# First four attention groups of a fused attention and two-MLP kernel: products with v by chunks of 32 keys in four PSUM banks, a new start order, one load of mem_v

## The chip, the cores and the metric

The kernel runs on one core of one Trainium2 chip. The metric is the device time of one execution in microseconds (us). Before the change it was 1058.13 us, the median of three runs (1057.98 to 1058.34).

## What is computed

Attention over chunks: 4 sequences, 8 heads, 768 tokens, 64 values a head. Each chunk of 32 queries sees its own 32 keys, 16 to the left, 8 to the right and 8 memory keys, so 64 keys in all. Two MLPs follow on the 3072 tokens.

```python
for c in range(nc):                               # chunks of 32 queries
    k_full = np.concatenate([mem_k, k_ctx], axis=2)
    v_full = np.concatenate([mem_v, v_ctx], axis=2)
    scores = scale * np.matmul(q_c, k_full.transpose(0, 1, 3, 2))
    a = np.exp(scores - np.max(scores, axis=-1, keepdims=True))
    a = a / (np.sum(a, axis=-1, keepdims=True) + 1e-09)
    out[:, :, c_start:c_end] = np.matmul(a, v_full)
h = x @ w_in                                      # 512 to 2048
x = np.where(h > 0.0, h, np.exp(np.minimum(h, 0.0)) - 1.0) @ w_out
y = ((x @ w1) * (x @ w2)) @ w3 @ w_out2
```

## The kernel before, in words

The work goes in 24 groups of 128 queries (four chunks, eight heads). Six matrices' worth of weights come as 64-bit numbers and are taken apart into a high and a low 32-bit part on ScalarE and VectorE; a product of such parts is three matmuls (`mm3`, lines 130 to 133). The first MLP runs by blocks of 512 tokens, which is four groups. So before the first matmul of the first MLP (`mm_h(0)`, lines 602 to 608) the first four groups (0 to 3) must have gone through attention. This start is written out by hand in the string `START` (line 72): a letter is a step, a digit its group, and every engine executes its instructions in the order in which the string issues them.

The steps of a group: `t` (351) transposes q and k on TensorE and copies them to SBUF; `s` (372) multiplies them to scores, 32 matmuls that the trace shows as 64 records; `m` (391) takes the maximum and subtracts it on VectorE, then exponentiates on ScalarE; `z` (400) sums and inverts; `n` (411) multiplies by the inverse; `p` (423) transposes by blocks of 32 on VectorE; `v` (429) multiplies with v; `o` (439) splits the result into a cast (ScalarE, line 127) and a remainder (VectorE, line 128) for the MLP. `k` and `w` ask for the q, k and v of a group on the SyncE queue (299 to 328), and the `l` steps ask for weights (147, 155). A group's v comes as one load of 128 tokens (line 321), four of 24 tokens (325) and, in groups 0 to 2, four of the 8 memory values (328, on the GpSimd queue).

In `n` the probabilities of 32 keys are written twice, once as they are and once as zeros, with the factors `rc` that line 406 makes with the mask `odd`. So `p` moves 1024 elements a partition, and `v` takes the keys in two blocks of 64 rows, for two chunks at a time, the zeros cancelling the other chunk's keys: 32 matmuls of 64 rows, 64 columns of v and 64 moving columns (64 records).

The weights go through `Feed` (204 to 263). One `act` (letter `a`) does on ScalarE the high part of job i-2 (line 179), the rebase of job i (166) and its top bits (188); one `dve` (letter `d`, in two halves `x` and `y`) does on VectorE the low part of job i-3 (182) and the merge of job i-1 (192). `act` also asks for the load of a later job. `mm_h(0)` needs both parts of job 0, and line 914 issues the steps that are still missing. The letters `i` and `j` are 6 matmuls each whose result nobody reads (`busy`, 595), shown as 12 records each.

PSUM has eight banks: `PA` (two), a pair for group 1 and one for group 2, and `PS[4]`, `PS[5]`. After the start the pairs' room becomes `PS[0]` to `PS[3]`. Groups 1 and 2 have their own SBUF tiles.

Of the kernel before, what the change touches and what calls it, by code (L numbers as in the profile page):

```python
# [8 lines left out]
F32 = mybir.dt.float32  # L9
# [4 lines left out]
ALU = mybir.AluOpType  # L14
# [6 lines left out]
def tile_kernel(  # L21
# [23 lines left out]
    nc = tc.nc  # L45
    P = 128
    B, H, S, D = q.shape
    NM = mem_k.shape[2]
    CH, LEFT, RIGHT = 32, 16, 8
    WIN = LEFT + CH + RIGHT  # L50
    KEYS = WIN + NM
    NCG = 4
    GQ = NCG * CH
    GPS = S // GQ
    NG = B * GPS
    HP = H // 2
    DM = H * D
    KT = DM // P
# [4 lines left out]
    EARLY = 3  # L63
# [5 lines left out]
    LATER = (11, 12, 13, 14, 15, 27, 28, 29, 30, 31)  # L69
    SHARED = {2: 24, 3: 25, 4: 26}  # L70

    START = "u0 t0 b1 k3 w1 l2 w2 s0 m0 t1 b2 s1 z0 n0 m1 t2 p0 v0 w3 l4 l6 c s2 z1 n1 o0 m2 p1 t3 v1 k4 s3 z2 n2 p2 o1 a d a m3 d v2 i z3 j n3 p3 o2 a d x v3 o3 a y w4"
    SCALE = 1.0 / float(D) ** 0.5
    assert GQ == P and KEYS == 64 and KT == 4 and HP == 4 and DM == 512

# [2 lines left out]
    psum = ctx.enter_context(tc.tile_pool(name="psum", bufs=1, space=PSUM))  # L78
# [5 lines left out]
    ident = const.tile([P, P], F32, name="ident")  # L84
    xhl = [const.tile([P, 2, KT, TB], F32R, name=f"xhl{i}") for i in range(2)]
# [1 line left out]
    for i, j in SHARED.items():  # L87
        W[j] = W[i]
    PA = psum.tile([P, 2, 512], F32, name="banks")
    PS = [None if i < KT else psum.tile([P, 512], F32, name=f"bank{i}") for i in range(6)]  # L90
    early_psum = ctx.enter_context(ExitStack())
    pb_p = early_psum.enter_context(tc.tile_pool(name="pb_p", bufs=1, space=PSUM))
    PB = [pb_p.tile([P, 2, 512], F32, name=f"pair{i}") for i in range(EARLY - 1)]

    w3d = [[dram.tile([P, 2, 512], F32, name=f"w3d{h}_{c}") for c in range(FF2)] for h in range(2)]
    wod = [dram.tile([P, 2, 512], F32, name=f"wod{c}") for c in range(FF2)]
# [21 lines left out]
    mm = nc.tensor.matmul  # L118
# [154 lines left out]
    def at_tile(G, pool, shape, name, tag=None):  # L273
        tag = tag or name
        if 0 < G < EARLY:
            pool, tag = early_p, f"{tag}{G}"
        return pool.tile(shape, F32, tag=tag, name=name, bufs=1)
# [8 lines left out]
    odd = at_tile(0, at_p, [GQ, 2, 1], "odd")  # L286

    def banks(G):
        return PB[G - 1] if 0 < G < EARLY else PA

    def small(shape, name):
        return at_p.tile(shape, F32, tag=name, name=name, bufs=2)
# [1 line left out]
    def by_token(src, b, t0, t1):  # L294
        return src[b, :, t0:t1, :].rearrange("h s d -> s h d")
# [3 lines left out]
    def load_qk(G):  # L299
        if G >= NG:  # L300
            return
        b, g = divmod(G, GPS)
        t0 = g * GQ + RIGHT
        n = min(P, S - t0)
        kn_g = k_t[G] = at_tile(G, qk_p, [P, H, D], "kn") if 0 < G < EARLY else kn
        q_t[G] = at_tile(G, qk_p, [GQ, H, D], "qn")
        if g == 0:
            nc.sync.dma_start(out=head[0:RIGHT], in_=by_token(k, b, 0, RIGHT))
            nc.sync.dma_start(out=head[RIGHT:RIGHT + NM], in_=by_token(mem_k, b, 0, NM))
        eng = nc.scalar if G == 0 else nc.sync  # L310
        eng.dma_start(out=q_t[G], in_=by_token(q, b, g * GQ, (g + 1) * GQ))
        nc.sync.dma_start(out=kn_g[0:n], in_=by_token(k, b, t0, t0 + n))

    def load_v(G):
        if G >= NG:
            return
        b, g = divmod(G, GPS)
        t0 = g * GQ - LEFT
        p0 = max(0, -t0)
        vw_g = v_t[G] = at_tile(G, v_p, [P, 2, H, D], "vw") if 0 < G < EARLY else vw  # L320
        nc.sync.dma_start(out=vw_g[p0:P, 0], in_=by_token(v, b, t0 + p0, t0 + P))
        for c in range(NCG):
            t1 = t0 + (c + 1) * CH
            n1 = min(LEFT + RIGHT, S - t1)
            nc.sync.dma_start(out=vw_g[c * CH:c * CH + n1, 1], in_=by_token(v, b, t1, t1 + n1))
            if g == 0 or G < EARLY:
                eng = nc.gpsimd if G < EARLY else nc.sync
                eng.dma_start(out=vw_g[c * CH + LEFT + RIGHT:(c + 1) * CH, 1], in_=by_token(mem_v, b, 0, NM))

    def bank(G, r, b):  # L330
        return banks(G)[:, r, 0:HP * b].rearrange("p (a b) -> p a b", b=b)
# [18 lines left out]

    def at_turn(G):
        qn, kn, pq, pk = q_t.pop(G), k_t.pop(G), bank(G, 0, GQ), bank(G, 1, P)
        for hp in range(HP):
            nc.tensor.transpose(pq[:, hp, :], pair(qn, hp), ident)  # L354
        for hp in range(HP):
            nc.tensor.transpose(pk[:, hp, :], pair(kn, hp), ident)  # L356
        qT = at_tile(G, at_p, [P, HP, GQ], "qT", "qp")
        if G not in kT_t:
            at_border(G)
        kT = kT_t[G]  # L360
        blocks = pk.rearrange("p a (c k) -> p a c k", k=CH)
        copy_on("v" if G < 2 else "a", qT, pq)
        nc.scalar.copy(kT[:, :, :, FRONT:WIN], blocks)
        nc.scalar.copy(kT[:, :, 1:NCG, 0:FRONT], blocks[:, :, 0:NCG - 1, CH - FRONT:CH])
        if G % GPS < GPS - 1:
            nc.scalar.copy(front[:, :, 0, :], blocks[:, :, NCG - 1, CH - FRONT:CH])
        qT_t[G] = qT
# [32 lines left out]
    def at_sum(G):  # L400
        rc = small([GQ, 2, 2 * HP], "rc")
        sm = small([GQ, 1, 2 * HP], "sm")
        nc.vector.tensor_reduce(out=sm, in_=e_t[G], axis=AX, op=ALU.add)
        nc.vector.tensor_scalar_add(sm, sm, 1e-9)
        nc.vector.reciprocal(out=sm, in_=sm)
        nc.vector.tensor_tensor(
            out=rc, in0=sm.to_broadcast([GQ, 2, 2 * HP]), in1=odd.to_broadcast([GQ, 2, 2 * HP]), op=ALU.mult
        )
        e_t[G] = e_t[G], rc

    def at_norm(G):
        e, rc = e_t[G]
        e2 = at_tile(G, at_p, [GQ, 2 * HP, 2, 2, CH], "e2", "qp")
        for s in range(2):
            nc.vector.tensor_tensor(
                out=e2[:, :, :, s, :],
                in0=e.rearrange("p r a (u k) -> p (r a) u k", u=2),
                in1=rc[:, s].rearrange("p (a u k) -> p a u k", u=1, k=1).to_broadcast([GQ, 2 * HP, 2, CH]),
                op=ALU.mult,
            )  # L420
        e_t[G] = e2

    def at_flip(G):
        e2 = e_t.pop(G)
        pT = at_tile(G, at_p, [P, 2, HP, 2, 2 * CH], "pT", "ke")
        nc.vector.transpose(out=pT.rearrange("p r a u i -> p (r a u i)"), in_=e2.rearrange("p a u s k -> p (a u s k)"))  # L426
        pT_t[G] = pT

    def at_values(G):
        pT, vw, px = pT_t.pop(G), v_t.pop(G), banks(G)  # L430
        for hp in range(HP):
            for u in range(2):
                for c in range(2):
                    cc = slice(c * D, (c + 1) * D)
                    for r in range(2):
                        o = px[r * D:(r + 1) * D, c, hp * D:(hp + 1) * D]
                        mm(o, lhsT=vw[cc, u, 2 * hp + r, :], rhs=pT[cc, r, hp, u, :], start=u == 0, stop=u == 1)  # L437

    def at_out(G):
        px = banks(G)[:, :, 0:2 * GQ].rearrange("p x (a t) -> p x a t", a=HP)  # L440
        j, g = divmod(G, GPB)
        hi, lo = (
            xhl[j % 2][:, i, :, g * GQ:(g + 1) * GQ].rearrange("p a (x t) -> p x a t", x=2) for i in range(2)
        )
        split(hi, lo, px)

# [123 lines left out]
    for G in range(GPB, NG):  # L570
        s0 = base(G)
# [22 lines left out]

    def busy(x, times):
        for _ in range(times):
            mm(PS[5][0:2 * H, 0:P], lhsT=x, rhs=ident, start=True, stop=True)

    h_t, eg_t, g_t = {}, {}, {}
    seq = [(j, f, f, f == FF1 - 1) for j in range(NB) for f in range(FF1)]  # L600
# [220 lines left out]
    with tc.manual_schedule():  # L821
# [10 lines left out]
        first_late = min(due[i] for i in LATER)  # L832
        feed = Feed(jobs)

        nc.gpsimd.memset(front, 0.0)
        load_qk(0)
        nc.scalar.copy(memo, front[:, :, :, 0:NM])
        make_identity(nc, ident)
        nc.gpsimd.memset(vw[0:LEFT, 0], 0.0)
        for c in range(NCG):  # L840
            for s in range(2):
                nc.gpsimd.memset(odd[c * CH:(c + 1) * CH, s], float(c % 2 == s))
        load_qk(1)
        load_qk(2)
        load_v(0)
        one = dict(t=at_turn, b=at_border, u=at_first, s=at_scores, m=at_max, z=at_sum, n=at_norm, p=at_flip, v=at_values, o=at_out, k=load_qk, w=load_v)
        for what in START.split():
            if what == "a":
                feed.act()
            elif what == "d":  # L850
                feed.dve()
            elif what == "x":
                feed.low_part()
            elif what == "y":
                feed.merge_part()
            elif what == "i":
                busy(ident[:, 0:2 * H], 6)
            elif what == "j":
                busy(e_t[3][1].rearrange("p s a -> p (s a)"), 6)
            elif what == "c":  # L860
                feed.cap = len(jobs)
            elif what[0] == "l":
                feed.cap = int(what[1])
                feed.load(feed.cap)
            else:
                one[what[0]](int(what[1]))
        assert feed.at == feed.acted
        early_psum.close()
        psum_x = ctx.enter_context(tc.tile_pool(name="psum_x", bufs=1, space=PSUM))
        for i in range(KT):  # L870
            PS[i] = psum_x.tile([P, 512], F32, name=f"bank{i}")
        NH = NB * FF1
        for n in range(NH + 2):
# [173 lines left out]
```

## Time and profile before

| | |
|---|---|
| median of three runs | 1058.13 us (1057.98 to 1058.34) |
| the profiled execution, its own time | 1057.77 us |
| its span, first to last instruction | 1056.0 us |
| TensorE busy over the span | 1033.5 us (98%) |
| VectorE, ScalarE busy | 566.8 us (54%), 458.6 us (43%) |
| GpSimd busy | 8.5 us, all in the first 10 us |
| first matmul of the first MLP | 36.31 us after the start |

The profiled execution lies 0.36 us below the median. TensorE is the bound over nearly all of the span, and its idle time lies at the start and at the very end; all that the diff touches lies in the first 37 us. So the question is at what time the dense part begins. A line of a timeline gives the start, the length, the engine, the line of the kernel, the operation, the tiles and shapes and how many instructions were merged; in brackets stands the idle time before it and what ended that.

### The profile page before, as it was taken

The page shows a single profiled execution, that of the slowest core. Times are in us where ns is not written, and L with a number is a line of the kernel's source. Part 1 is how long each engine was busy: PE and PEld are TensorE (multiplying, and loading weights), DVE is VectorE, ACT ScalarE, POOL GpSimd, SP SyncE. Part 2 cuts the span into 40 slices and gives each one's busy share as a digit, 9 for nine tenths or more (in the row PEclk, how much of TensorE's full clock was granted, in tenths as well). Part 3 has the DMA queues.
Part 4 walks back from the last instruction along what each step waited for, and adds up shares of the span by engine and source line. Part 5 has one row for each costly group of instructions (what it writes and reads, how often), then busy time and mean ns, then how long its engine had stood idle before and what let it go on. Part 6 is the DMA issues. An engine that isn't in the chain of part 4 may idle for free.

```text
span 1056.0 us, 19258 instructions
## 1 busy us (share of the span) xinstructions
PE 1033.5 (98%) x7784; PEld 884.8 (84%) x7784; DVE 566.8 (54%) x989; ACT 458.6 (43%) x890; POOL 8.5 (1%) x28
## 2 busy tenths in 40 slices
PE   5899999999999999999999999999999999999997
PEld 4678888888888888888888888899999999999996
DVE  6898856657665756666572324144444444444323
ACT  4888755545555555455543332122222223222222
POOL 3000000000000000000000000000000000000000
PEclk9999999999999999999999999999999999999999
DMA  9998648565856675667536645554475466546521
GB/s 179 268 268 250 185 141 264 158 208 179 239 161 210 194 219 183 205 193 236 163 140 212 238 159 160 174 182 162 151 271 169 157 216 231 162 141 220 169 70 61
DMA packets 178005, 199.19 MB, mean 189 GB/s; under 512 B 101404, under 2 KB 142620, under 8 KB 177916
## 3 DMA queue, kind: packets, MB, share of 16 engines
q1 hardware_dynamic: 176348, 197.36, 60.3%
q8 instruction: 62, 1.02, 0.4%
q10 hardware_dynamic: 1184, 0.39, 0.1%
q0 software_dynamic: 384, 0.20, 0.1%
q14 instruction: 27, 0.22, 0.1%
HBM read 154.93 MB, written 42.99 MB: 187 GB/s over the span
## 4 chain that ended last, share of the span: by engine, by line
PE 95%; DVE 2%; ACT 2%; DMA 1%; issue 0%; SPq 0%; DVEq 0%; ACTq 0%
PE bank L131 21%; PE bank L133 20%; PE bank L132 20%; PE bank L740 7%; PE bank L741 7%; PE bank L739 7%; PE banks L437 2%; PE banks L133 2%; PE banks L132 2%; PE banks L131 2%; PE banks L378 2%; PE banks L356 1%; PE banks L354 1%; PE banks L472 1%; DMA raw<-in_moe_w_in_dram 0%; DVE pT L426 0%
## 5 line engine op out<-in xcount | busy, mean ns | idle before, releaser
L131 PE MATMUL bank<-xhl,w 128*128 128x512 f32 x384 | 153.9, 401 | 1.0 <-ACT xhl L127 1.0
L131 PE MATMUL bank<-g,w 128*128 128x512 f32 x384 | 153.3, 399 | 0.0
L133 PE MATMUL bank<-g,w 128*128 128x512 f32 x384 | 150.0, 391 | 0.0
L132 PE MATMUL bank<-xhl,w 128*128 128x512 f32 x384 | 149.8, 390 | 0.2 <-DVE xhl L128 0.2
L133 PE MATMUL bank<-xhl,w 128*128 128x512 f32 x384 | 150.0, 391 | 0.0
L132 PE MATMUL bank<-g,w 128*128 128x512 f32 x384 | 149.8, 390 | 0.0
L612 ACT ACTIVATE eg<-bank 128x512 f32<-128x512 f32 x96 | 57.3, 597 | 116.1 <-PE bank L133 115.8
L618 DVE SCALAR_TENSOR_TENSOR eg<-eg,bank 128x512 f32<-128x512 f32 x96 | 65.6, 684 | 66.3 <-ACT eg L613 66.3
L504 DVE TENSOR_TENSOR e<-bank,e 128x384 f32<-128x384 f32 x64 | 35.7, 558 | 119.2 <-PE bank L741 119.2
L131 PEld LDWEIGHTS bank<-xhl,w 128*128 128x128 f32 x384 | 72.1, 188 | 16.1 <-ACT xhl L127 1.1
L131 PEld LDWEIGHTS bank<-g,w 128*128 128x128 f32 x384 | 72.1, 188 | 15.6
L133 PEld LDWEIGHTS bank<-xhl,w 128*128 128x128 f32 x384 | 72.1, 188 | 15.6
L133 PEld LDWEIGHTS bank<-g,w 128*128 128x128 f32 x384 | 72.1, 188 | 15.3
L132 PEld LDWEIGHTS bank<-xhl,w 128*128 128x128 f32 x384 | 72.2, 188 | 14.5 <-DVE xhl L128 0.5
L132 PEld LDWEIGHTS bank<-g,w 128*128 128x128 f32 x384 | 72.2, 188 | 14.3 <-DVE g L626 0.3
L626 DVE TENSOR_TENSOR g<-eg,g 128x512 fp32r<-128x512 f32 x96 | 65.9, 686 | 21.7 <-ACT g L622 21.5
L740 PE MATMUL bank<-xd,w 128*128 128x384 f32 x224 | 75.8, 338 | 0.0
L622 ACT CAST g<-eg 128x512 fp32r<-128x512 f32 x96 | 59.7, 622 | 28.2 <-DVE eg L618 28.0
L504 DVE TENSOR_TENSOR e<-bank,eg 128x384 f32<-128x384 f32 x64 | 35.7, 557 | 58.8 <-PE bank L741 58.8
L741 PE MATMUL bank<-xd,w 128*128 128x384 f32 x192 | 64.7, 337 | 0.0
L739 PE MATMUL bank<-xd,w 128*128 128x384 f32 x192 | 64.2, 334 | 0.0
L613 ACT ACTIVATE eg<-eg 128x512 f32<-128x512 f32 x96 | 60.7, 633 | 3.1
(173 smaller groups left out, 1855.1 us busy)
## 6 DMA issues: line engine op xcount, KB each, us to landing
w<-wqd SPq DMA_DIRECT2D x96, 512.0 KB
raw<-in_moe_w_dram SPq DMA_DIRECT2D x32, 512.0 KB
w<-shd SPq DMA_DIRECT2D x30, 512.0 KB
wqd<-st SPq DMA_DIRECT2D x24, 512.0 KB
raw<-in_moe_w_out_dram SPq DMA_DIRECT2D x22, 512.0 KB
w3d<-st SPq DMA_DIRECT2D x16, 512.0 KB
w<-w3d SPq DMA_DIRECT2D x16, 512.0 KB
w<-wqd SPq DMA_DIRECT2D x32, 256.0 KB
```

Source lines behind the costliest of these rows:

```text
L131: mm(o, lhsT=w_hi, rhs=x_hi, start=start, stop=False)
L132: mm(o, lhsT=w_hi, rhs=x_lo, start=False, stop=False)
L133: mm(o, lhsT=w_lo, rhs=x_hi, start=False, stop=stop)
L504: nc.vector.tensor_tensor(out=o, in0=a, in1=b, op=op)
L612: nc.scalar.activation(e, h_t[n], AF.Relu, scale=-1.0)
L613: nc.scalar.activation(e, e, AF.Exp, scale=-1.0)
L618: nc.vector.scalar_tensor_tensor(out=e, in0=e, scalar=-1.0, in1=h_t.pop(n), op0=ALU.add, op1=ALU.max)
L622: nc.scalar.copy(g_t[n][:, 0, :], eg_t[n])
L626: nc.vector.tensor_tensor(out=g[:, 1, :], in0=eg_t.pop(n), in1=g[:, 0, :].bitcast(F32), op=ALU.subtract)
L739: mm(o, lhsT=args[0], rhs=args[2], start=start and i == 0, stop=False, skip_group_check=more)
L740: mm(o, lhsT=args[0], rhs=args[3], start=False, stop=False, skip_group_check=more)
L741: mm(o, lhsT=args[1], rhs=args[2], start=False, stop=i == 1, skip_group_check=more)
```

## The change

1. `v` in groups 0 to 3: the probabilities stay as they are, without zeros. `n` is one multiply of 512 elements, `p` transposes 512 elements, line 406 is gone, and `v` multiplies each chunk of 32 keys for itself: 64 matmuls of 32 rows, 64 columns of v and 32 moving columns, each chunk into a bank of its own (`PV`, four banks shared by the four groups). The output is read from four banks.
2. PSUM: groups 0 and 2 use `PA`, groups 1 and 3 one pair `PB`. The transposed q of groups 0 and 1 goes to `PV`, that of 2 and 3 stays beside k. `PS[4]` and `PS[5]` come only after the start, and the matmuls of `i` and `j` write to `PA`.
3. mem_v is loaded once (four loads on the ScalarE queue), into the tile of group 1, which VectorE clears first; GpSimd copies it to the tiles of groups 0 and 2. The twelve loads on the GpSimd queue are gone.
4. Order: `p0` stands before `m1`, `p1` before `o0`; one `a d` less stands before `m3`, so that each remaining `a` and `d` works on an earlier job, and the missing step is issued by line 914 just before `mm_h(0)`; `n3` stands before `j`, which now reads the result of `n3`.

```diff
-    START = "u0 t0 b1 k3 w1 l2 w2 s0 m0 t1 b2 s1 z0 n0 m1 t2 p0 v0 w3 l4 l6 c s2 z1 n1 o0 m2 p1 t3 v1 k4 s3 z2 n2 p2 o1 a d a m3 d v2 i z3 j n3 p3 o2 a d x v3 o3 a y w4"
+    START = "u0 t0 b1 k3 w1 l2 w2 s0 m0 t1 b2 s1 z0 n0 p0 m1 t2 v0 w3 l4 l6 c s2 z1 n1 p1 o0 m2 t3 v1 k4 s3 z2 n2 p2 o1 a m3 d v2 i z3 n3 j p3 o2 a d x v3 o3 a y w4"
...
-    PS = [None if i < KT else psum.tile([P, 512], F32, name=f"bank{i}") for i in range(6)]
+    PS = [None] * 6
...
-    PB = [pb_p.tile([P, 2, 512], F32, name=f"pair{i}") for i in range(EARLY - 1)]
+    PB = pb_p.tile([P, 2, 512], F32, name="pair")
+    PV = pb_p.tile([P, NCG, 512], F32, name="four")
...
-        return PB[G - 1] if 0 < G < EARLY else PA
+        return PB if G in (1, EARLY) else PA
...
+    def load_mem_v(eng, vw_g, b, c):
+        eng.dma_start(out=vw_g[c * CH + LEFT + RIGHT:(c + 1) * CH, 1], in_=by_token(mem_v, b, 0, NM))
...
-            if g == 0 or G < EARLY:
-                eng = nc.gpsimd if G < EARLY else nc.sync
-                eng.dma_start(out=vw_g[c * CH + LEFT + RIGHT:(c + 1) * CH, 1], in_=by_token(mem_v, b, 0, NM))
+            if g == 0 and G:
+                load_mem_v(nc.sync, vw_g, b, c)
...
+        if G < 2:
+            pq = PV[:, G].rearrange("p (a b) -> p a b", b=GQ)
...
+        if G <= EARLY:
+            e2 = e_t[G] = at_tile(G, at_p, [GQ, 2 * HP, 2, CH], "e2", "qp")
+            nc.vector.tensor_tensor(
+                out=e2,
+                in0=e.rearrange("p r a (u k) -> p (r a) u k", u=2),
+                in1=rc.rearrange("p s (a u k) -> p (s a) u k", u=1, k=1).to_broadcast([GQ, 2 * HP, 2, CH]),
+                op=ALU.mult,
+            )
+            return
...
+        if G <= EARLY:
+            for hp in range(HP):
+                for u in range(2):
+                    for c in range(NCG):
+                        cc = slice(c * CH, (c + 1) * CH)
+                        for r in range(2):
+                            o = PV[r * D:(r + 1) * D, c, hp * CH:(hp + 1) * CH]
+                            mm(o, lhsT=vw[cc, u, 2 * hp + r, :], rhs=pT[cc, r, hp, u, :], start=u == 0, stop=u == 1)
+            return
...
-            mm(PS[5][0:2 * H, 0:P], lhsT=x, rhs=ident, start=True, stop=True)
+            mm(PA[0:2 * H, 0, 0:P], lhsT=x, rhs=ident, start=True, stop=True)
...
+        vw_early = [vw] + [at_tile(G, v_p, [P, 2, H, D], "vw") for G in range(1, EARLY)]
+        nc.vector.memset(vw_early[1][:, 1], 0.0)
...
+        for c in range(NCG):
+            load_mem_v(nc.scalar, vw_early[1], 0, c)
...
+        for i in (0, 2):
+            nc.gpsimd.tensor_copy(vw_early[i][:, 1], vw_early[1][:, 1])
...
-                busy(e_t[3][1].rearrange("p s a -> p (s a)"), 6)
+                busy(e_t[3].rearrange("p a u k -> p (a u k)")[:, 0:2 * H], 6)
...
-        for i in range(KT):
+        for i in (4, 5, 0, 1, 2, 3):
             PS[i] = psum_x.tile([P, 512], F32, name=f"bank{i}")
```

## Rows read from the trace of the kernel before

**Rows 1.** Windows: busy time and instructions by engine, then clock, DMA share, GB/s.

```profile
...
120.00:200.00 80.00, 80.00 (x722) 65.10 (x722) 51.99 (x95) 43.24 (x84) 0.00 (x0) 1.00 0.60 182
...
```

**Rows 2.** The chain of work that ended last, in order of time, 0 to 70 us.

```profile
...
29.40 5.10 DMA raw<-in_moe_w_in_dram
...
48.53 0.69 DVE f L192
...
59.34 1.28 PE banks L437 x64
...
```

**Rows 3.** Timeline of PE, 0 to 62 us.

```profile
...
19.45 0.86 PE L378 MATMUL pair<-kT,qT 64*32 64x64 f32 x64
...
23.58 2.22 PE L437 MATMUL pair<-pT,vw 64*64 64x64 f32 x64 [1.38 <-DVE pT L426]
25.74 1.18 PE L378 MATMUL banks<-kT,qT 64*32 64x64 f32 x64
...
29.26 1.03 PE L437 MATMUL pair<-pT,vw 64*64 64x64 f32 x52 [0.31 <-DMA vw<-in_v_dram]
30.22 1.48 PE L597 MATMUL bank<-ident 128*16 128x128 f32 x12
31.54 1.47 PE L597 MATMUL bank<-ident,rc 128*16 128x128 f32 x12
34.04 1.28 PE L437 MATMUL banks<-pT,vw 64*64 64x64 f32 x64 [1.03 <-DVE pT L426]
36.31 0.50 PE L131 MATMUL bank<-xhl,w 128*128 128x512 f32 x1 [0.99 <-ACT xhl L127]
...
40.84 0.66 PE L356 MATMUL banks<-ident,kn 128*128 128x128 f32 x4 [0.39 <-DMA kn<-in_k_dram]
...
```

**Rows 4.** Groups of instructions by line and shape, 0 to 37 us: busy us, mean ns.

```profile
...
L415 DVE TENSOR_TENSOR e<-e,rc 128x512 f32<-128x512 f32 x8 | 5.2, 688 | 0.1
L426 DVE STREAM_TRANSPOSE pT<-e 128x1024 f32<-128x1024 f32 x4 | 5.0, 1240 | 0.1
...
```

**Rows 5.** Timeline of ACT, 0 to 62 us.

```profile
...
0.75 0.43 ACTq L311 DMA_DIRECT2D qn<-in_q_dram  x1
...
34.52 0.71 ACT L166 ACTIVATE f<-raw 128x512 f32<-128x512 f32 x1 [3.09 <-DMA raw<-in_moe_w_in_dram]
...
35.67 0.59 ACT L127 CAST xhl<-banks 128x512 fp32r<-128x512 f32 x1
36.13 0.64 ACT L179 CAST w<-f 128x512 fp32r<-128x512 f32 x1
...
49.42 0.67 ACT L166 ACTIVATE f<-raw 128x512 f32<-128x512 f32 x1
...
```

**Rows 6.** DMA queues, 0 to 50 us (packets, MB, share), and the issues by line.

```profile
...
q0 software_dynamic: 384, 0.20, 2.8%
...
vw<-in_mem_v_dram POOLq DMA_DIRECT2D x12, 16.0 KB, 5.2
...
```

**Rows 7.** Windows of 4 us, the columns of rows 1.

```profile
...
8.00:12.00 4.00, 3.02 (x72) 2.51 (x72) 1.55 (x3) 1.39 (x5) 1.85 (x4) 1.00 1.37 182
...
20.00:24.00 4.00, 1.82 (x50) 1.42 (x36) 3.97 (x6) 1.65 (x6) 0.00 (x0) 0.98 0.88 264
24.00:28.00 4.00, 3.18 (x128) 2.80 (x127) 3.83 (x9) 3.05 (x7) 0.00 (x0) 0.59 0.84 174
28.00:32.00 4.00, 3.16 (x80) 2.74 (x74) 3.65 (x8) 2.39 (x5) 0.00 (x0) 1.00 0.61 141
...
```

**Rows 8.** Timeline of DVE, 0 to 62 us.

```profile
...
7.17 0.69 DVE L124 COPY qT<-banks 128x512 f32<-128x512 f32 x1 [7.17 <-PE banks L356]
...
32.74 1.25 DVE L426 STREAM_TRANSPOSE pT<-e 128x1024 f32<-128x1024 f32 x1
...
```

**Rows 9.** Timeline of POOL, 0 to 62 us.

```profile
...
1.38 0.51 POOL L839 MEMSET vw<- 16x512 f32 x1
...
```

**Rows 10.** Timeline of the SyncE queue, 0 to 62 us.

```profile
...
8.98 2.67 SPq L325 DMA_DIRECT2D vw<-in_v_dram  x4
...
```

More of the change, by code (lines that the diff above doesn't have):

```diff
@@ L319, in load_v @@
         p0 = max(0, -t0)
-        vw_g = v_t[G] = at_tile(G, v_p, [P, 2, H, D], "vw") if 0 < G < EARLY else vw
+        vw_g = v_t[G] = vw_early[G] if G < EARLY else vw
         nc.sync.dma_start(out=vw_g[p0:P, 0], in_=by_token(v, b, t0 + p0, t0 + P))
@@ L405, in at_sum @@
         nc.vector.reciprocal(out=sm, in_=sm)
+        if G <= EARLY:
+            e_t[G] = e_t[G], sm
+            return
         nc.vector.tensor_tensor(
@@ L424, in at_flip @@
         e2 = e_t.pop(G)
+        if G <= EARLY:
+            pT = pT_t[G] = at_tile(G, at_p, [P, 2, HP, 2, CH], "pT", "ke")
+            nc.vector.transpose(out=pT.rearrange("p r a u i -> p (r a u i)"), in_=e2.rearrange("p a u k -> p (a u k)"))
+            return
         pT = at_tile(G, at_p, [P, 2, HP, 2, 2 * CH], "pT", "ke")
@@ L430, in at_values @@
         pT, vw, px = pT_t.pop(G), v_t.pop(G), banks(G)
+        if G <= EARLY:
+            for hp in range(HP):
[5 more added lines that the diff above has]
+                            mm(o, lhsT=vw[cc, u, 2 * hp + r, :], rhs=pT[cc, r, hp, u, :], start=u == 0, stop=u == 1)
+            return
         for hp in range(HP):
@@ L439, in at_out @@
     def at_out(G):
-        px = banks(G)[:, :, 0:2 * GQ].rearrange("p x (a t) -> p x a t", a=HP)
+        n = NCG if G <= EARLY else 2
+        px = (PV if G <= EARLY else banks(G))[:, :, 0:DM // n].rearrange("p x (a t) -> p x a t", a=HP)
         j, g = divmod(G, GPB)
         hi, lo = (
-            xhl[j % 2][:, i, :, g * GQ:(g + 1) * GQ].rearrange("p a (x t) -> p x a t", x=2) for i in range(2)
+            xhl[j % 2][:, i, :, g * GQ:(g + 1) * GQ].rearrange("p a (x t) -> p x a t", x=n) for i in range(2)
         )
```

## The prediction, made blind

> **What bounds the kernel now.** I read the windows first. From 120 to 200 us TensorE is busy 80.00 of 80.00 us [rows 1], so nothing that the change does can be seen there: it can only move the time at which this dense part begins. Then I read the chain of waits. It goes through a weight's transfer from 29.40 to 34.5 us, then without a gap through ScalarE to 48.5 us, through VectorE, and reaches TensorE with the product with v of group 4 at 59.34 us [rows 2]. So between 34.5 and 59 us not TensorE but the ScalarE and VectorE work is late, and a step that moves on ScalarE at 36 us moves the whole rest. Last I read the timelines of the start. TensorE's second product (group 2) runs its last part only at 29.26 us, when the last of its v has landed [rows 3]. VectorE is busy nearly without a break: 3.97, 3.83 and 3.65 of 4 us [rows 7].
>
> **VectorE, part by part.** The multiply by the inverse is done eight times in the four groups, 688 ns each; four of them go, 2.75 us. The transpose takes 1240 ns for 1024 elements [rows 4]; for 512 I take half and a little, 0.65 us (bounds 0.62 and 1.24), so 4 x 0.59 = 2.4 us go. With the four small mask products that makes some 5 us. Group 3's transpose, which began at 32.74 us [rows 8], would end near 29. It doesn't follow that the start ends 5 us earlier: group 2's v still lands where the transfers let it, and what is late next is that transfer. So I cost the VectorE saving at nothing. The earlier q and k copies (PV lets VectorE and ScalarE read different tiles) save under 1 us before the first scores and go to the same wait. Clearing the one v tile (0.2 to 0.7 us) lies in VectorE's idle 7.17 us at the start [rows 8].
>
> **The transfers.** Twelve loads of 16 KB go, 0.20 MB [rows 6], and four come, 0.066 MB. The queues run full there: the DMA share is 1.37 and 182 GB/s are moved [rows 7]. 0.131 MB at 182 GB/s are 0.72 us; by the number of packets it is a little more, and I take 0.8 us (bounds 0 and 1.5) by which all later loads land earlier. The four issues on ScalarE cost 0.43 us each [rows 5], 1.7 us in a stretch in which it waits for the first transposes. The two GpSimd copies are of 512 elements; its clearing of 512 took 0.51 us [rows 9], and I take 0.5 to 1.2 us each. They must end before SyncE may ask for the tails of v (line 325), first at 8.98 us [rows 10]; mem_v is asked for by about 5 us and took 5.2 us to land on the old queue [rows 6]. A wait of a microsecond or two there is covered by the loads that are already queued.
>
> **The products.** Each has 128 records in place of 64. Nothing in the trace has 32 rows. The nearest row is the scores: 64 columns move, over eight places in the array as in the new product, and 64 records take 0.86 us, 13.4 ns each [rows 3]. The old product has four places and takes 1.28 us, 20 ns each [rows 3]. I take 13.4 ns, so 1.72 us a product: 0.44 us dearer than before. Bounds are 10 ns (less streams in each) and 20 ns (each record costs what it cost).
>
> [...]
>
> **The path to the first MLP.** Group 2's v has landed at 29.26 - 0.8 = 28.46 us. Behind it are 112 of 128 records: 1.50 us, to 29.96. Then `i` and `j`, which run from 30.22 to 33.01 us, 2.79 us [rows 3], stand ahead of group 3's product: that starts at 32.75 instead of 34.04. (Its wait for the bank that group 2's cast and remainder read, 1.3 us, and its transposed input are covered by `i` and `j`; so is the later `n3`.) It ends at 34.47, and its cast starts at 34.53, 1.14 us earlier than the 35.67 of before [rows 5].
>
> Now the moved `a d`. Before, rebase and top bits of the third job stood ahead of the cast, from 34.52 us, and the high part of the second job followed at 36.13 [rows 5]. After, behind the cast come the high part of the first job, then rebase and top bits of the third, then the second's high part. The same three plus one more: 34.53 + 0.46 + 0.52 + 1.15 = 36.66 us instead of 36.13, **0.5 us later** on the ScalarE chain that the rest hangs on. VectorE gets one merge and one low part between the cast and the third matmul of the first MLP, which comes near 37.0; the first stood at 36.31 [rows 3]. TensorE itself would be ready: group 4's keys, for which it waited until 40.84 [rows 3], land earlier too. But the gain there is lost in the wait for ScalarE. The weights' loads that `act` asks for come one step later, so one goes behind group 4's five loads of v on the SyncE queue. Its rebase stands at 49.42 us [rows 5], some 10 us after the asking, and I cost the delay at nothing (up to 0.5 us if that cover is gone).
>
> **The clock.** [...] After, TensorE is done with group 3's scores by some 24.3 us (25.74 + 1.18 = 26.92 before [rows 3], less half of VectorE's 5 us) and has next to nothing until v lands at 28.46. [...]
>
> **The sum,** at the end of the ScalarE work that stands around group 3's cast: -0.8 (v lands earlier), +0.54 (behind it 1.50 us of the second product instead of 30.22 - 29.26 = 0.96), -1.03 (no wait between `j` and group 3's product, 33.01 to 34.04), +0.15 (that product and the step to its cast, 1.78 instead of 1.63), which is the cast's -1.14; +0.52 (one more high part behind the cast), +1.15 (rebase and top bits behind it instead of ahead): +0.5. With 0.4 for the clock: +0.9 us. The profiled execution took 1057.77 us, 0.36 below the median; set against the median, 1058.13 + 0.9 = **1059.0 us**. A measurement of this kernel tells 0.2%, 2.1 us, from no change, so the forecast is no difference.
>
> **Rivals.** (a) *The clock stays down over `i` and `j`* (slower). [...] It decides if the low clock lasts beyond about 31 us. [...] Against it: before, the clock was back while TensorE ran one product and one set of scores. 15%.
> (b) *A record of the product costs 20 ns whatever its size* (slower). The two products on the path take 112 x 20 and 128 x 20 ns, 0.74 and 0.84 us more than summed: +2.1 to +2.5, 1060.4. The scores speak against it; that they load 32 columns of weights and the product 64 speaks for it. 12%. [...]
> (c) *Transfers and products both at their good ends* (faster). 1.5 us earlier and 10 ns a record: 0.7 and 0.8 us off the 0.5, -1.0 us: 1057.1. It decides if group 2's v lands by 27.8 us. Against it: only 0.13 MB go. 20%, with 4% for more than 2.1 us.
> (d) *SyncE waits for the GpSimd copies* until the queued loads run dry (slower). I put those at 3 us (an estimate: the first four tails alone took 2.67 us to ask for [rows 10]); if the copies end after 12 us, each further microsecond moves all loads: about +1, 1060.0. 7%.
>
> **The numbers.** The forecast has 46%, with its own range 1057.9 to 1060.0. Slower by over 0.2%: most of (a) and half of (b), with a little of (d) and of the forecast, 20%. Faster by over 0.2%: 4%. The range reaches from (c) without its far end to (a) with a clock that returns late: 1056.9 to 1061.3.
>
> **What would show it.** Right: in the changed profile group 2's product waits for a transfer of v near 28.5 us, group 3's transpose is done before 30, group 3's product follows `j` without a wait, and the chain still reaches group 4's product, near 60 us, through ScalarE. The three steps are shown wrong by a product that takes over 2.2 us at the full clock, by v landing at 29.2 as before, or by group 4's product earlier than 59. A first MLP matmul before 34 us would make the whole prediction wrong.

## The result: slower, by more in most runs than in the profiled one

The changed kernel took 1064.07 us in the median of six runs (1060.83 to 1066.74), the kernel before 1058.03: a ratio of 1.0056, interval 1.0047 to 1.0066, some 6 us. That is outside the predicted range (1056.9 to 1061.3). The kernel before stays within 1.1 us over its six runs, the changed one spreads over 5.9. The profiled execution, 1060.83 us, is the fastest of the six, so its profile shows about half of the usual loss: +3.06 us against the profiled execution before.

The first section of the profile's page after, here for TensorE: 256 matmul records more than the 7784 of before, four groups with 64 each (and as many weight loads).

```profile
PE 1037.9 (98%) x8040; PEld 888.7 (84%) x8040; DVE 562.9 (53%) x982; ACT 458.8 (43%) x890; POOL 2.9 (0%) x18
```

The timeline of TensorE after, which answers to [rows 3]:

```profile
16.35 1.95 PE L459 MATMUL four<-pT,vw 32*64 32x32 f32 x128
18.48 0.86 PE L383 MATMUL banks<-kT,qT 64*32 64x64 f32 x64 [0.18 <-ACT front L371]
...
22.66 1.01 PE L359 MATMUL pair<-ident,qn 128*128 128x128 f32 x4 [3.32 <-issue]
...
24.46 2.47 PE L459 MATMUL four<-pT,vw 32*64 32x32 f32 x128
26.86 1.18 PE L383 MATMUL pair<-kT,qT 64*32 64x64 f32 x64
28.36 1.10 PE L459 MATMUL four<-pT,vw 32*64 32x32 f32 x55 [0.32 <-DVE xhl L129]
30.15 1.34 PE L459 MATMUL four<-pT,vw 32*64 32x32 f32 x73 [0.70 <-issue]
31.42 2.56 PE L628 MATMUL banks<-ident 128*16 128x128 f32 x12
33.81 1.47 PE L628 MATMUL banks<-ident,e 128*16 128x128 f32 x12
35.22 0.45 PE L459 MATMUL four<-pT,vw 32*64 32x32 f32 x30
35.95 1.18 PE L459 MATMUL four<-pT,vw 32*64 32x32 f32 x98 [0.28 <-issue]
```

Look at the idle times marked "issue": 3.32, 0.70 and 0.28 us in which the profile shows nothing that TensorE waited for. Two of them cut a product in the middle. Now count between them. Beside each matmul record the trace has a record of its weight load, so 128 matmul records are 256 records in all. From 22.66 to the cut at 30.15: 4 + 4 (group 3's k, not in the fence) + 128 + 64 + 55 = 255 matmul records, 510 with the weight loads. From there to the cut at 35.95: 73 + 12 + 12 + 30 = 127, so 254. So the cuts lie 254 records and twice 255 apart; I call what lies between two such places a block. The profile's list of DMA queues agrees: in q8, which it marks "instruction", from 0 to 40 us, four transfers of 16 KB before, six after. Over the whole execution they are 62 before and 64 after, two more for TensorE's 512 records more, so 256 records a transfer; the other queue with that mark, q14, has 27 in both.

```profile
q8 instruction: 4, 0.07, 0.8%
```

```profile
q8 instruction: 6, 0.10, 1.3%
```

The windows after, with the columns of [rows 1], show a second thing, the granted clock (third column from the end). It is at 0.50 from 20 to 32 us, where before only 24 to 28 us lay low (mean 0.59 [rows 7]), and low again under the first MLP matmuls (mean 0.57 from 40 to 44 us).

```profile
20.00:24.00 4.00, 1.34 (x7) 1.34 (x7) 3.08 (x7) 0.99 (x3) 0.00 (x0) 0.50 0.93 278
24.00:28.00 4.00, 3.96 (x195) 3.22 (x193) 1.30 (x3) 2.53 (x6) 0.00 (x0) 0.50 0.72 139
28.00:32.00 4.00, 2.98 (x134) 2.59 (x132) 3.08 (x7) 1.80 (x4) 0.00 (x0) 0.50 0.89 257
32.00:36.00 4.00, 3.72 (x61) 2.75 (x58) 2.14 (x4) 1.24 (x3) 0.00 (x0) 0.79 0.83 265
40.00:44.00 4.00, 4.00 (x12) 3.03 (x13) 2.97 (x5) 4.00 (x9) 0.00 (x0) 0.57 1.04 300
```

The path then goes as the prediction read it, through ScalarE. First group 3's cast and the first exponent step of the MLP after (line 643), then that step before (line 612):

```profile
37.27 0.58 ACT L128 CAST xhl<-four 128x512 fp32r<-128x512 f32 x1 [4.03 <-PE four L459]
...
44.35 0.58 ACT L643 ACTIVATE eg<-bank 128x512 f32<-128x512 f32 x1
```

```profile
41.07 0.58 ACT L612 ACTIVATE eg<-bank 128x512 f32<-128x512 f32 x1
```

And group 4's product with v comes at 62.73 us instead of 59.34 [rows 2], +3.39, of which the span keeps 3.0:

```profile
62.73 1.28 PE L467 MATMUL banks<-pT,vw 64*64 64x64 f32 x64 [0.53 <-DVE pT L447]
```

### The profile page after: what moved, and what is told of

Its sections match the earlier page's. It is cut to its first block, busy times and chain, and to the rows that moved or that the text cites. A ratio compares the mean times of both kernels' runs of the same rounds, so it can differ in the third digit from the quotient of the medians.

```text
span 1059.0 us, 19734 instructions
## 1 busy us (share of the span) xinstructions
PE 1037.9 (98%) x8040; PEld 888.7 (84%) x8040; DVE 562.9 (53%) x982; ACT 458.8 (43%) x890; POOL 2.9 (0%) x18
## 4 chain that ended last, share of the span: by engine, by line
PE 95%; DVE 2%; ACT 2%; issue 1%; DMA 0%; SPq 0%; ACTq 0%; DVEq 0%
PE bank L132 21%; PE bank L134 20%; PE bank L133 20%; PE bank L771 7%; PE bank L772 7%; PE bank L770 7%; PE banks L467 2%; PE banks L134 2%; PE banks L133 2%; PE banks L132 2%; PE banks L383 2%; PE banks L361 1%; PE banks L359 1%; PE banks L503 1%; PE four L459 1%
```

## The experiments

Two theories to tell apart: the *supply* of TensorE's instructions, which the doubled records of the products outrun, and the *order* of the start (with the shared banks), whose moved `a d` was the cost that the prediction had named. Each ratio is against runs of the kernel before on the same chip. The edits are abridged: `...` and comments stand for what is left out.

### Old products, all else changed (e1)

```diff
-        if G <= EARLY:      # sums, multiply, transpose, product by 32 keys
-            ...
+        # the old path: 64 rows with zeros, 64 records, two banks of PV
```

> The changed kernel with the old products in groups 0 to 3 (64 rows with zeros, 64 records a group, two of the four banks of PV); order, PSUM, the one load of mem_v stay changed. Supply theory (TensorE's instructions come in blocks of 256 records, and the doubled records of the products outrun them): the stretch without work ahead of group 3's transposes (19.3 to 22.7 us) shrinks to under 1 us, group 4's product comes before 60 us, and the time is 1057 to 1059 us. Order theory (the moved a d and the shared banks cost the time): still 1060 or more.

Measured: 1061.06 us, ratio 1.0028 (1.0017 to 1.0039), within 0.7 us over six runs. The spread is gone and group 3's transposes follow the scores without a stretch; one cut of 0.69 us is left, inside group 1's product. But 3 us remain, and group 4's product comes at 62.25 us: so neither theory has it all. The cast starts 1.27 us later than before (35.67 [rows 5]). As the timelines read, with `p0` and `p1` moved forward nothing fills VectorE's wait for the exponents, and group 3's product then waits 0.97 us for group 2's remainder. From the cast to line 620, the exponent step, 7.06 us pass instead of 5.40, which is the moved `a d`.

```profile
36.94 0.59 ACT L128 CAST xhl<-four 128x512 fp32r<-128x512 f32 x1 [4.15 <-PE four L444]
...
44.00 0.57 ACT L620 ACTIVATE eg<-bank 128x512 f32<-128x512 f32 x1
```

### The kernel before with its records doubled (e2)

```diff
-                        o = px[r * D:(r + 1) * D, c, hp * D:(hp + 1) * D]
-                        mm(o, lhsT=vw[cc, u, 2 * hp + r, :], rhs=pT[cc, r, hp, u, :], start=u == 0, stop=u == 1)
+                        # groups 0 to 3, for h in range(2), outside u
+                        o = px[r * D:(r + 1) * D, c, hp * D + h * CH:hp * D + (h + 1) * CH]
+                        mm(o, lhsT=vw[cc, u, 2 * hp + r, :], rhs=pT[cc, r, hp, u, h * CH:(h + 1) * CH], start=u == 0, stop=u == 1)
```

> The kernel before, with each product of groups 0 to 3 issued as two matmuls of 32 moving columns instead of one of 64: the same arithmetic, rows and zeros, 128 records a group instead of 64, nothing else changed. Supply theory: stretches without work open on TensorE at every 256th record, between 19 and 36 us, the clock falls for longer, and the time goes up by 2 to 7 us. Order theory: at most 1 us, for the products' own length.

Measured: 1070.46 us, ratio 1.0112 (1.0099 to 1.0125), +12.6 us: more than the supply theory's upper end. The records' own length explains a part of it: group 3's product took 2.07 us for 128 records instead of 1.28, so four products cost some 3 us. The cuts are where the count puts them:

```profile
31.68 0.64 PE L440 MATMUL pair<-pT,vw 64*64 64x32 f32 x12 [0.85 <-issue]
32.25 1.18 PE L378 MATMUL banks<-kT,qT 64*32 64x64 f32 x64
33.36 1.70 PE L440 MATMUL pair<-pT,vw 64*64 64x32 f32 x50
38.67 2.35 PE L440 MATMUL pair<-pT,vw 64*64 64x32 f32 x78 [3.61 <-issue]
40.96 2.74 PE L608 MATMUL bank<-ident 128*16 128x128 f32 x12
```

12 + 64 + 50 = 126 matmul records, 252 with the weight loads, so nearly one block; then 3.61 us of nothing inside group 2's product. Only the number of records and their length (32 moving columns instead of 64) were changed here. (`i` took 2.74 us, nearly twice its 1.48 of [rows 3], though this profile's windows from 0 to 120 us show the clock at 1.00 throughout; that is left open.)

### The changed kernel with half of its records (e8)

```diff
-                for u in range(2):
+                for u in range(1):
...
-                            mm(o, lhsT=vw[cc, u, 2 * hp + r, :], rhs=pT[cc, r, hp, u, :], start=u == 0, stop=u == 1)
+                            mm(o, lhsT=vw[cc, u, 2 * hp + r, :], rhs=pT[cc, r, hp, u, :], start=True, stop=True)
```

> The changed kernel with the products of groups 0 to 3 leaving out the second 32 keys (64 records a group instead of 128); VectorE, order, PSUM, loads as changed. Leaves out part of the sum over keys. Supply theory: no stretch without work over 1 us ahead of group 3's transposes, the runs lie within 1 us of one another, and what is left is what the blind prediction summed without the third cost, 1058 to 1060 us. If the stalls had another cause than the number of records, the time stays at 1061 to 1067 with the same spread.

Measured: 1058.62 us, ratio 0.9998 (0.9989 to 1.0007). The 6 us are gone with half of the records, VectorE, order and loads being as changed. The runs spread over 3 us (1057.45 to 1060.49), not 1, but so did 29 runs of the kernel before on this chip, over 2.7. One cut of 1.11 us is left inside group 1's product. Its profile comes nearest to what the prediction had in mind:

```profile
26.86 1.17 PE L459 MATMUL four<-pT,vw 32*64 32x32 f32 x64 [2.30 <-DMA vw<-in_v_dram]
27.96 2.74 PE L628 MATMUL banks<-ident 128*16 128x128 f32 x12
30.49 2.24 PE L628 MATMUL banks<-ident,e 128*16 128x128 f32 x12
32.66 0.86 PE L459 MATMUL four<-pT,vw 32*64 32x32 f32 x64
```

Group 2's product waits for v, and v is there at 26.86 us, 2.4 us earlier than before. Around and after that wait the clock is low (mean 0.65 from 24 to 28 us, 0.50 from 28 to 32), and `i` and `j` take 4.77 us instead of 2.79. The kernel also leaves out the work of those records, about 0.9 us a product at 13.4 ns each, so not all of its 6 us are waiting.

### The stretch follows the count (e10)

```diff
+        busy(ident[:, 0:2 * H], 10)
         for what in START.split():
```

> The changed kernel with ten matmuls more (40 records, results unread) at the very start, where TensorE waits for the first keys. Supply theory: the stretches without work stand where the 256-record blocks end, so each moves 40 records forward: the one before group 3's transposes (record 706 of the changed profile) now lies inside group 2's scores, about 40 of their 128 records from the end; the time stays at 1061 to 1067. If the stretch belonged to the transposes (a wait for data or a bank), it stays where it was.

Measured: 1064.29 us, ratio 1.0059 (1.0045 to 1.0072). The stretch left the transposes and now cuts group 2's scores, 19 matmuls (38 records) from their end, and the transposes follow at once:

```profile
18.45 0.69 PE L383 MATMUL banks<-kT,qT 64*32 64x64 f32 x45
23.94 0.63 PE L383 MATMUL banks<-kT,qT 64*32 64x64 f32 x19 [4.80 <-issue]
24.50 1.11 PE L359 MATMUL pair<-ident,qn 128*128 128x128 f32 x4
```

In the start of the kernel before, no set of scores shows a wait once it has begun (64 records in 0.86 and in 1.18 us, without a gap [rows 3]). So the stretch belongs to the place in the instruction stream and not to a step. The other profiles agree: counted from the start of the program, every cut marked "issue" inside a step stands at matmul record 221, 346 to 349, 472 to 476, 598 to 603 or 730, whatever step is there. (The mark "issue" alone is not enough: the kernel before has 1.02 us of it ahead of group 0's product, which starts at 18.01 us, when VectorE's transpose has just ended.)

Beside the stretches stand the packets of q8 in the traces, the blocks counted as above. Times in us:

| stretch ends in | block's end before it crossed | next transfer of 16 KB starts | has landed | TensorE goes on |
|---|---|---|---|---|
| changed, group 3's transposes | 17.45 | 18.55 | 21.33 | 22.66 |
| changed, group 2's product | 26.49 | 27.62 | 28.73 | 30.15 |
| e2, group 2's product | 31.68 | 36.30 | 37.35 | 38.67 |
| e4, group 2's product | 27.84 | 33.16 | 34.09 | 35.62 |
| e10, group 2's scores | 17.46 | 21.20 | 22.23 | 23.94 |

Each transfer starts only after the last block's end was crossed. At all such cuts in the profiles TensorE goes on 0.8 to 1.8 us after a transfer has landed. Most transfers take 0.9 to 1.6 us (three took 2.2 to 2.9); what varies most is how long after the crossing they start, 0.8 to 5.3 us. So I read the stretches as TensorE's wait for that transfer.

### The order: old order with the new products (e5) and with the old ones (e6)

```diff
-    START = "... z0 n0 p0 m1 t2 v0 ... z1 n1 p1 o0 m2 t3 v1 ... o1 a m3 d v2 i z3 n3 j p3 ..."
+    START = "... z0 n0 m1 t2 p0 v0 ... z1 n1 o0 m2 p1 t3 v1 ... o1 a d a m3 d v2 i z3 n3 j p3 ..."   # e5; e6 has j n3
```

> The changed kernel with the start order of before (only n3 stays ahead of j). Supply theory: the stretches without work on TensorE stay, the runs still spread by 3 us or more, and the time is about 1.5 to 3 us under the changed kernel's, which is the order's own cost: 1061 to 1063. If the order alone were the cause: 1057 to 1058.

Measured: 1065.14 us, ratio 1.0055 (1.0042 to 1.0067): the old order gives nothing back while the records are doubled, against an expected 1.5 to 3 us. This profile is of a run of 1065.28 us, a usual one. It suggests where the changed kernel's median loses what its profiled run, the fastest, did not (no usual run of that kernel was profiled): 3.45 us inside group 2's product, where that one had 0.70.

```profile
34.62 1.33 PE L459 MATMUL four<-pT,vw 32*64 32x32 f32 x73 [3.45 <-issue]
```

> Old products and old start order, with the changed PSUM and the one load of mem_v. The run with old products and new order took 3.2 us more than the kernel before. Order theory for that run: those 3.2 us go, and the earlier loads give up to 1 us: 1057 to 1058.3 us. If PSUM sharing or the loads cost them: 1060 or more.

Measured: 1058.37 us, ratio 0.9997 (0.9989 to 1.0006). With the old products, the old order takes back all of e1's 3.2 us, and the PSUM change and the one load of mem_v cost nothing that can be measured. The two costs do not add: the order takes 3.2 us alone (e1), the records some 6 without the moved order (e5), and both together some 6. They gain nothing either: `i` and `j` took 5.07 us instead of 2.79 (mean clock over the execution 0.994, before 0.998), and group 3's product came at 35.08 us, later than the 34.04 of [rows 3].

```profile
30.08 2.74 PE L605 MATMUL banks<-ident 128*16 128x128 f32 x12
32.61 2.54 PE L605 MATMUL banks<-ident,rc 128*16 128x128 f32 x12
35.08 1.16 PE L444 MATMUL four<-pT,vw 64*64 64x64 f32 x64
```

### The a d put back (e3)

```diff
-    START = "... o1 a m3 d v2 ..."
+    START = "... o1 a d a m3 d v2 ..."
```

> The changed kernel with the a d that the change took out put back (a d a m3 d). My prediction's term: ScalarE's extra work behind group 3's cast goes, 0.5 us less than the changed kernel. Order theory: 2 us or more less. Supply theory: the stretch ahead of group 3's transposes stays, and the time stays within 1 us of the changed kernel's.

Measured: 1062.47 us (1059.37 to 1066.06), ratio 1.0046 (1.0028 to 1.0064), against 1.0056 for the changed kernel: the intervals overlap, so this alone decides nothing.

### Without i and j (e4)

```diff
-    START = "... d v2 i z3 n3 j p3 ..."
+    START = "... d v2 z3 n3 p3 ..."
```

> The changed kernel without the 12 matmuls of i and j. If they lie on the path at the low clock (3.8 us from 31.4 to 35.2 in the changed profile), group 3's product starts 1.5 to 2 us earlier and the time falls by 1 to 2 us, unless the clock then falls again under the first matmuls of the MLP, which would give up to 2 us back. Supply theory: the stretch ahead of group 3's transposes is there as before.

Measured: 1063.84 us, ratio 1.0055 (1.0043 to 1.0067), no gain. In its profile a stretch of 4.41 us stands ahead of group 3's transposes, group 2's product is cut for 4.82 us, and the clock stays low under the MLP (mean 0.50 from 40 to 44 us, 0.83 from 44 to 48):

```profile
35.62 1.34 PE L459 MATMUL four<-pT,vw 32*64 32x32 f32 x73 [4.82 <-issue]
38.36 2.25 PE L459 MATMUL four<-pT,vw 32*64 32x32 f32 x128 [1.40 <-DVE xhl L129]
```

### The first weights' loads behind v (e11)

```diff
-    START = "... w1 l2 w2 ..."
+    START = "... w1 w2 ..."      # l4, behind w3, asks for them
```

> The changed kernel with the first two weights' loads (1 MB) asked for behind group 3's v instead of ahead of group 2's. If a block of instructions comes late because its transfer stands behind those loads, the block that took 2.8 us from 18.6 us on is there by 20.5, the stretch ahead of group 3's transposes is under 1.5 us, and the time falls by 2 us or more, less what the later weights cost (0 to 2 us). If the block's delay does not depend on the data traffic: the stretch stays at 2 us or more.

Measured: 1065.55 us, ratio 1.0066 (1.0054 to 1.0079). The stretch ahead of group 3's transposes was 1.80 us, between the two expectations, and e3's was 1.83 with the loads where they were; the later cut was 2.43 us. The block's transfer took 1.31 us and had landed at 20.44, but e4's took 1.15 with the loads where they were. So it is not shown that those loads hold up the blocks. The profile puts the 1.80 us down to VectorE's line 401; but in e8 the same transposes start before that step does (19.05 against 20.44 us), so they don't wait for it.

```profile
21.83 1.01 PE L359 MATMUL pair<-ident,qn 128*128 128x128 f32 x4 [1.80 <-DVE e L401]
```

### Towards a version that is faster than both (e7, e12, e9)

```diff
-        if G <= EARLY:              # by 32 keys in groups 0 to 3
+        if G in SPLIT:              # e7, e12: SPLIT = (3,), group 3 alone, old order
...
-                busy(ident[:, 0:2 * H], 6)
+                busy(ident[:, 0:2 * H], 3)      # e12, e9, and the same in j
```

> As the run of the old order, but only group 3's product is by chunks of 32 keys; groups 0 to 2 have 64 records. VectorE saves 1.2 us where its chain is last, and only 64 records are added, at the end. Supply theory: no spread, and 1056.5 to 1058, at or under the kernel before. Against it: a stall of 1 us or more in group 3's own product, 1058 to 1060.

Measured: 1059.87 us, ratio 1.0010 (1.0002 to 1.0019), runs from 1057.64 to 1061.67, so not at or under the kernel before. They spread over 4.0 us, against 2.7 of the kernel before on the same chip. The one product with doubled records is cut, too, in this profile of a fast run (1058.30 us) only for 0.32 us:

```profile
34.58 0.57 PE L462 MATMUL four<-pT,vw 32*64 32x32 f32 x35 [0.32 <-issue]
```

> As the run with only group 3 by chunks, with 3 matmuls in i and in j. Group 3's input is ready earlier there than with old products, so more of the shorter i and j shows: 1 to 2 us under that run, 1057 to 1059, unless its product then meets the end of a block (0.3 us in that run, up to 2 us here) or a low clock.

Measured: 1062.36 us, ratio 1.0035 (1.0023 to 1.0047), slower than e7 and than expected. Shorter `i` and `j` made it worse: with 24 records fewer in a row, the same product is cut 12 matmul records further on, and for 3.14 us.

```profile
39.03 0.65 PE L462 MATMUL four<-pT,vw 32*64 32x32 f32 x23 [3.14 <-issue]
```

> Old products, old order, changed PSUM and loads (the run of parts 2 and 3), with 3 matmuls in i and in j instead of 6. In that run i and j took 5.0 us at the low clock and group 3's product followed them. If they are on its path, group 3's product starts up to 2 us earlier and the time falls by 0.5 to 2 us, under the kernel before; if the clock stays low longer for it, 0 to 2 us more.

Measured: 1060.17 us, ratio 1.0010 (1.0001 to 1.0019), against e6's 0.9997 (0.9989 to 1.0006): some 1.4 us more by the ratios, though the intervals just overlap. Group 3's product started 1.0 us earlier than in e6 (34.11) but took 2.01 us instead of 1.16, at the low clock (0.50 from 32 to 40 us), which lasted over the MLP's first matmuls (mean 0.70 from 40 to 44). None of the three is faster than the kernel before.

## Why the prediction was wrong, step by step

- **What bounds the kernel: right.** All happens before group 4's product, and after the cast the delay passes through ScalarE to it without loss: the cast is 1.60 us later (37.27 against 35.67 [rows 5]), the exponent step 3.28 (44.35 against 41.07), the product 3.39.
- **VectorE at nothing, but for the wait of 1.03 us: right as far as seen.** The transpose of 512 took 0.71 us (0.65 was taken). In e8, where VectorE's saving is whole, group 3's input is ready at 29.78 us and its product follows `j` without a wait, as the sum has it.
- **The transfers, -0.8: too small.** The last v was there 1.5 us earlier in e7 (27.74) and 2.4 earlier in e8 (26.86), at and beyond the bound of 1.5. Of e8's 2.4 us, 0.28 were left at the end of `j` (32.73 against 33.01), because `i` and `j` took 1.98 us more, at a clock of 0.50 from 28 to 32 us. Rival (c), which hung on this landing, did not come. The changed kernel's product of group 2 did start near the forecast 28.5 us (28.36), but by luck: it waited not for v but for VectorE's remainder of group 1.
- **The products: right in price, and here the prediction failed.** 13.4 ns a record was right (98 records in 1.18 us at a clock of 1.00, 12.0 ns; 73 in 1.34 at 0.50, 18.4 ns, as the scores of before in the low window, 64 in 1.18 us, 18.5 ns [rows 3]). The step "I take 13.4 ns, so 1.72 us a product" assumed that TensorE has its instructions when it wants them. 128 records of a product with their weight loads are 256 records, a whole block by the counts above (254 to 256). The sum had no term for that, and none of the rivals did; e2, e8, e10 and the landings of the blocks show that this is what brings the stretches of 0.3 to 4.8 us. Between e8 and the changed kernel, the doubled records make the 6 us; the low clock and their own 0.9 us a product are in it.
- **Group 3's product at 32.75 and its cast at 34.53: wrong by 2.5 and 2.7 us** (35.22 and 37.27) in the profiled run, by the stretches ahead of group 3's transposes and inside group 2's product (3.32 and 0.70 us) and by the low clock (0.50 from 20 to 32 us). In e8 the cast starts at 33.55, 2.1 us earlier than before; the moved `a d` then takes most of that back.
- **The moved a d, +1.67 us between the cast and what hangs on it: right.** 7.08 us instead of 5.40, +1.68; 7.06 in e1, and 5.43 with the old order in e6. That it is the order that costs when the records are not doubled is shown by e1 and e6 together, 1.0028 against 0.9997, both with the old products; in e8, whose VectorE work is shorter, the new order costs nothing in all. Of the 2.23 us between their profiled runs 1.63 lie behind the cast, with the `a d`, and 0.60 ahead of it, with the moved `p` steps; the two were not tried apart.
- **The clock: too weak.** Rival (a), the low clock over `i` and `j`, given 15%, came true. They took 3.86 us (31.42 to 35.28; clock 0.50 up to 32 us, mean 0.79 from 32 to 36) instead of 2.79, and 4.77 in e8 (0.50 from 28 to 32), with half the records: so it does not need the doubled records. In e8 2.30 us of waiting for v stand ahead of group 2's product and 1.11 us inside group 1's; which of the two brings it, or neither, was not tried. The 0.4 us that the sum takes for the clock was my estimate and no run shows it; what the runs show is `i` and `j` dearer by 1.07 us after and by 1.98 in e8.
- **Rivals (b) and (d) did not come.** The GpSimd copies ended at 8.9 us (7.70 + 1.16), and SyncE asked for the first tails of v at 8.34, earlier than the 8.98 of before [rows 10].

What stays open: how much of the 6 us is waiting for blocks and how much the low clock, since in the changed kernel's profile they come together (the stretch of 3.32 us ends at 22.66 us, the clock is at 0.50 from 20 us on); and why a block is late by 0.3 us in one run and 4 in another. The traces say that this lies mostly in when the block's transfer starts, not in how long it takes; what holds up the start is not shown.

## What to carry to other kernels

When a change multiplies small matmuls, count instructions as well as their lengths: here 254 to 256 records, weight loads included, made one block, and a stretch that ran through a block in a few us could stand still at its end (for 3.32 us after one that began at 17.45 and ended near 19.3). An idle time marked "issue" that cuts a loop of equal matmuls in the middle, at equal counts from the last such cut, pointed to that here; twenty matmul records more at the start of the program, which moved the cut by 19, tested it (e10). And the transfer that landed earlier was worth little with the clock at 0.50 over the work behind the wait (0.28 of 2.4 us in e8).

## What the runs showed that I had not expected

- The instruction stream held TensorE up for microseconds in a kernel that runs it at 98%: 4.82 us at one block's end (e4), and with identical arithmetic +12.6 us for 256 matmul records more (e2).
- The same `i` and `j` took 2.79 us before, at a clock of 1.00, 3.86 after and 4.77 in e8, at 0.50 for a part or most of it, and 5.07 in e6. Yet leaving them out (e4) gained nothing, and halving them gained nothing either (e9, e12).
- The profile that happened to be taken was the fastest of six runs. The spread of the runs, 5.9 us against 1.1, hinted at something irregular in the path before any row did. It is a weak hint: beside the experiments the kernel before spread over 2.6 to 2.7 us, and e4, with cuts of over 4 us, over 1.5.
